# A normalization woven into a gated unit: one block for every four steps of dense work instead of three

## The chip, the cores and the metric

The kernel runs on one core of a Trainium2 chip. The metric is the device time of one execution in microseconds; of several executions the median counts. PE is the matmul engine (its weight loads are listed as PEld), DVE the vector engine, ACT the scalar engine, POOL the GpSimd engine, and SP issues most of the DMAs.

## The reference

The reference mixes two branches on one input `x` of 2048 rows and 640 columns, all in fp32:

```
g = sigmoid(sum(x * gate_w))                      # one number for each row
a = memory_attention(x; wq, wk, wv, wo, beta)     # 32 heads of 20, 4 chunks of 512 rows
b = (silu(x @ w1) * (x @ w3)) @ w2                # 1728 hidden columns
return g * a + (1 - g) * b
```

Within a chunk the attention is causal softmax over the chunk's own 512 rows. Beside it each chunk reads a memory, `phi(q) @ M / (phi(q) @ z)`, into which all earlier chunks have written `phi(k)^T @ v` and the sums of `phi(k)`. A sigmoid of `beta` mixes the two for each head, and `wo` projects the result.

## The kernel before, in words

The work is transposed: features lie on the 128 partitions and a chunk's 512 rows in the free dimension, so every matrix of 640 features has five blocks (`KB = 5`). For precision a factor is split into a high part and a low part, and a product is made of three matmuls per block of 128 (`PASSES`); a full product of one output block is 15 matmuls into one bank of PSUM. PSUM has eight banks, and all tiles in it are taken in turn from one list (`bank_tile`). A tile that gets a bank must wait until the last reader of the tile that had the bank before is done.

PE's order is the order in which the program is written; the other engines' instructions are ordered by a scheduler at build time. Two streams are merged into PE's order:

- The attention (`attention`, L761) goes over the heads in groups of four, in 40 slots each. In every group there is one big visit, with scores `s` (L602) for the row maxima, transposed scores `t` (L635) for the exponentials, and the product `o` (L655) with the values; and later a small visit with the rest of `s` and `t`. DVE reduces each `s` to row maxima (L609) and copies `o` out (L659). ACT makes the exponentials (L641), and POOL masks them (L645). After the small visit the maxima are split (L130 to L132), transposed on DVE (L620, `mr`) and sent into the next group's `qk` by two DMAs that ACT issues (L623).
- The dense work is a list of jobs, each a generator that yields after three matmuls or so, with the time in ns that they are reckoned at. A loop at the end of the kernel gives the dense jobs their share of each slot. At a big visit it first runs dense steps until no product is half done in its bank (`held` is empty).

The change concerns the segment of dense jobs that holds the output projection of the second chunk (chunk index 1). `ffn_up` (L502) is the gated unit: for one group of 128 hidden columns and the chunks 2 and 3 it makes a gate product `g` (15 matmuls, L253), a tanh on ACT (L514) and a product on DVE (L515), then an up product `u` (15 matmuls), a product on DVE (L521), a cast on ACT (L106) and the low part on POOL (L107). `normalize(1)` (L721) scales the attention output of chunk 1 block by block and adds the memory part; its loop is

```
ps = bank_tile(f"rr{c}_{b}")
nc.tensor.matmul(ps, sel[:, b * P:(b + 1) * P], rR, ...)     # L729: the factors, spread over rows
nc.vector.tensor_mul(o, oall[c][:, b].bitcast(F32), ps)      # L730
pt = bank_tile(f"gt{c}_{b}")                                 # L732
for qb in range(4):
    nc.tensor.transpose(pt[...], hi[...], ident)             # L734: the memory part, transposed
nc.vector.tensor_add(o, o, pt)                               # L735
nc.scalar.copy(hi, o)                                        # L736: high part, into gm
nc.vector.tensor_sub(oall[c][:, b], o, hi.bitcast(F32))      # L737: low part
yield 700
```

The output projection `op` (L805) then reads all five blocks of `gm` and `oall`, and is itself woven with the memory read `nd` (L348) of chunk 3. `braid(a, b, every)` (L856) merges two jobs: after every `every`-th step of `a` it runs one step of `b`, and at the end what is left of `b`. Weights are loaded by SP into two raw buffers (L163) and split on POOL (L174, L175) into six split buffers, each free when the last matmul on it is done.

## Time and profile before

| what | value |
|---|---|
| median of 3 runs | 1108.73 us (1108.67 to 1112.61) |
| the profiled execution | 1108.07 us, span 1106.4 us |
| granted clock of PE | 1.00 |
| matmul rows of the three dense products `g`, `u`, `f` | 840, 780, 820 |
| matmul rows of `s` and `o` | 512, 1024 |

In a row of the timeline stand the start in us from the span's start, the length in us, the engine, the line, the operation, the output and inputs by the program's names (without their numbers), the shape and the count of instructions merged; in brackets the engine's idle time just before and what ended it. The length of merged matmuls holds the tail of the last one, about 0.2 us, under which the next row has already begun. In a row of the waits stand who waited for whom, the sum in us, how often, and the longest. In a row of a stretch stand the stretch, its length, the busy times of PE, PEld, DVE, ACT and POOL with their counts, the granted clock, the share of the DMA engines and GB/s.

### The profile page before, as it was taken

What the parts mean: (1) busy time and instruction counts of PE and PEld (TensorE: products, weight loads), DVE (VectorE), ACT (ScalarE), POOL (GpSimd) and SP (SyncE); (2) the same over time, 40 slices, a digit from 0 to 9 for tenths busy, and PEclk for the clock granted to TensorE, in tenths of its full rate; (3) what the DMA queues carried; (4) which work ended last, traced back from release to release, by engine and by line L of the source; (5) the groups of instructions that cost most, each with busy time, mean ns of one, the idle gap of its engine ahead of it and who ended that gap; (6) DMA issues with size and microseconds to landing.
All of it is one profiled execution on the core that took longest, in us unless ns stands there. A gap on an engine that the chain in (4) does not pass through costs nothing.

```text
span 1106.4 us, 17867 instructions
## 1 busy us (share of the span) xinstructions
PE 1095.1 (99%) x6285; PEld 854.0 (77%) x6285; DVE 593.5 (54%) x1708; ACT 381.2 (34%) x826; POOL 583.3 (53%) x729
## 2 busy tenths in 40 slices
PE   9999999999999999999999999999999999999997
PEld 7988877777777777787977777777777777777786
DVE  5032564355555554366154678875557665551645
ACT  6244233343233122145244543424333332233120
POOL 5055556366366363565175547556764555565253
PEclk9999999999999999999999999999999999999999
DMA  8266943335165132535268967455654443432122
GB/s 314 102 212 220 281 117 82 95 82 127 47 164 125 57 78 94 156 98 191 96 202 271 287 204 193 103 157 138 166 139 111 103 104 90 117 105 86 52 79 95
DMA packets 87545, 153.20 MB, mean 138 GB/s; under 512 B 11584, under 2 KB 25184, under 8 KB 87456
## 3 DMA queue, kind: packets, MB, share of 16 engines
q1 hardware_dynamic: 63040, 106.30, 30.5%
q0 software_dynamic: 20384, 38.68, 15.6%
q10 hardware_dynamic: 4032, 7.08, 1.8%
q8 instruction: 50, 0.82, 0.3%
q14 instruction: 39, 0.32, 0.1%
HBM read 96.56 MB, written 54.54 MB: 137 GB/s over the span
## 4 chain that ended last, share of the span: by engine, by line
PE 94%; DVE 3%; ACT 1%; DMA 1%; issue 1%; ACTq 0%; SPq 0%; DVEq 0%
PE g L253 17%; PE u L253 16%; PE f L555 16%; PE k L253 6%; PE v L381 6%; PE op L805 6%; PE o L655 6%; PE q L253 5%; PE s L602 5%; PE t L635 4%; PE nd L348 1%; PE pm L445 1%; PE q L323 1%; DVE junk L609 1%; PE pkt L430 1%
## 5 line engine op out<-in xcount | busy, mean ns | idle before, releaser
L609 DVE CUSTOM_DVE_ANT_0 junk<-s,mask 128x256 bf16<-128x256 f32 (+3 forms) x512 | 250.3, 489 | 105.9 <-PE s L602 73.6
L641 ACT ACTIVATE P<-t 128x512 f32<-128x512 f32 (+1 forms) x384 | 172.4, 538 | 190.5 <-PE t L635 153.3
L253 PE MATMUL g<-X,W 128*128 128x512 f32 x840 | 208.7, 398 | 0.0
L175 POOL TENSOR_TENSOR W<-wr,W 128x640 fp32r<-128x640 f32 (+1 forms) x126 | 200.2, 1595 | 2.3
L174 POOL CAST W<-wr 128x640 fp32r<-128x640 f32 (+1 forms) x126 | 90.9, 726 | 208.9 <-PE f L555 47.0
L253 PE MATMUL u<-X,W 128*128 128x512 f32 x780 | 196.8, 399 | 0.0
L555 PE MATMUL f<-ht,W 128*128 128x512 f32 x820 | 196.6, 397 | 0.0
L645 POOL TENSOR_SCALAR_AFFINE_SELECT P<-P 128x256 f32<-128x256 f32 x192 | 94.0, 498 | 181.1 <-ACT P L641 180.7
L253 PEld LDWEIGHTS g<-X,W 128*128 128x128 f32 x840 | 156.0, 188 | 36.5 <-issue 0.4
L555 PEld LDWEIGHTS f<-ht,W 128*128 128x128 f32 x820 | 152.8, 188 | 36.5 <-DVE acc L536 0.4
L253 PEld LDWEIGHTS u<-X,W 128*128 128x128 f32 x780 | 144.1, 188 | 34.4 <-ACT P L641 0.3
L107 POOL TENSOR_TENSOR ht<-ft,ht 128x512 fp32r<-128x512 f32 x52 | 67.0, 1289 | 91.9 <-ACT ht L106 91.3
L579 POOL DMA_DIRECT2D qk<-qkd x128 | 83.3, 652 | 0.3
L602 PE MATMUL s<-qk 60*128 60x256 f32 (+3 forms) x512 | 78.2, 346 | 1.3 <-DVE fu L515 1.0
L253 PE MATMUL k<-X,W 128*128 128x512 f32 x300 | 77.0, 404 | 0.0
L655 PE MATMUL o<-P,vg 128*32 128x512 f32 (+3 forms) x1024 | 75.5, 436 | 1.4 <-DVE on L735 1.4
L514 ACT ACTIVATE ft<-g 128x512 f32<-128x512 f32 x52 | 31.1, 599 | 125.8 <-PE g L253 114.8
L381 PE MATMUL v<-W,X 128*128 128x320 f32 (+1 forms) x480 | 71.9, 311 | 0.4 <-ACT P L641 0.4
L515 DVE SCALAR_TENSOR_TENSOR fu<-ft,g 128x512 f32<-128x512 f32 x52 | 35.6, 685 | 68.3 <-ACT ft L514 59.2
L381 PEld LDWEIGHTS v<-W,X 128*128 128x128 f32 x480 | 71.0, 189 | 1.1 <-ACT P L641 0.6
L106 ACT CAST ht<-ft 128x512 fp32r<-128x512 f32 x52 | 32.2, 619 | 112.0 <-DVE ft L521 111.9
L563 DVE TENSOR_TENSOR acc<-f,acc 128x512 f32<-128x512 f32 x65 | 44.7, 689 | 44.8 <-PE f L555 44.6
(120 smaller groups left out, 1200.6 us busy)
## 6 DMA issues: line engine op xcount, KB each, us to landing
qk<-qkd POOLq DMA_DIRECT2D x128, 240.0 KB, 4.2
wr<-in_w_dram SPq DMA_DIRECT2D x80, 320.0 KB
qkd<-qs SPq DMA_DIRECT2D x20, 512.0 KB
qkd<-ks SPq DMA_DIRECT2D x20, 512.0 KB
od<-oq SPq DMA_DIRECT2D x32, 256.0 KB
wr<-in_wo_dram SPq DMA_DIRECT2D x20, 320.0 KB
vg<-vd SPq DMA_DIRECT2D x16, 336.0 KB
xr<-in_xT_dram SPq DMA_DIRECT2D x20, 256.0 KB
```

The source lines that it names most:

```text
L107: (lo or nc.gpsimd.tensor_sub)(dst[:, 1], src, dst[:, 0].bitcast(F32))
L174: nc.gpsimd.tensor_copy(w[:, 0, :n], raw[:, :n])
L175: nc.gpsimd.tensor_sub(w[:, 1, :n], raw[:, :n], w[:, 0, :n].bitcast(F32))
L253: nc.tensor.matmul(ps, w[:, a, kb * P:(kb + 1) * P], x[:, b, kb, :], start=n == 0, stop=n == 14)
L381: nc.tensor.matmul(ps[:, :n1 - n0], x[:, a, kb, lb * P:(lb + 1) * P], wvt[kb][:, b, n0:n1], start=n == 0, stop=n == 14)
L555: nc.tensor.matmul(ps, w, h, start=n == 0, stop=n == len(ms) - 1)
L579: here(nc.gpsimd.dma_start(t[64 * i:64 * i + RH], qkd[c][RH * (h + i):RH * (h + i + 1)]))
L602: nc.tensor.matmul(ps[i][:, o:o + w], q[:, qb * P:(qb + 1) * P], key[:, :w], start=n == 0, stop=n == len(todo) - 1, skip_group_check=True)
L609: nc.vector.tensor_tensor_reduce(out=junk[:, :w], in0=ps[i][:, o:o + w], in1=mask[:, L - w:], scale=1.0, scalar=-3.0e38, op0=ALU.add, op1= ...
L641: last["exp"] = nc.scalar.activation(pairs[2 * m + k]["P"][:, i, o:o + n], ps[i][:, b:b + n], AF.Exp, scale=SCALE)
L645: nc.gpsimd.affine_select(d, d, pattern=[[0, 2], [0, n], [1, P]], base=0, channel_multiplier=-1, compare_op=ALU.is_ge, fill=0.0)
L655: nc.tensor.matmul(ps[32 * i:32 * i + 32, kb * P:], heads[2 * p + i]["v"][:, kb], pairs[p + i // 2]["P"][:, i % 2, o:o + n], start=kb == 0 ...
```

## The change

In the segment of chunk 1's output projection, the gated unit `up[2]` of chunks 2 and 3 takes one block of `normalize(1)` after every four of its steps, where it took one after every three:

```
 o1, o2 = jobs_oproj(1)
-seg = [braid(up[2], o1, 3), braid(o2, job_read(3), 3, 1), job_down(B, 0), ...]
+seg = [braid(up[2], o1, 4), braid(o2, job_read(3), 3, 1), job_down(B, 0), ...]
```

`o1` is the normalization with its five blocks, `o2` the projection. Nothing else in the program is changed; what follows in the orders of the engines and in the turn of the banks follows from this number.

More of the change, by code (lines that the diff above doesn't have):

```diff
@@ L916, in gated_mix @@
     o1, o2 = jobs_oproj(1)
-    seg = [braid(up[2], o1, 3), braid(o2, job_read(3), 3, 1), job_down(B, 0), braid(chain(jobs_up(B, 1)), (0, load_memory(2)), 5)]
+    seg = [braid(up[2], o1, 4), braid(o2, job_read(3), 3, 1), job_down(B, 0), braid(chain(jobs_up(B, 1)), (0, load_memory(2)), 5)]
     segs.append((3 * H + LAG + 1, seg))
```

## The prediction

> **What bounds the kernel now.** I read the page first: its busy times and the chain that ended last.

> ```profile
> span 1106.4 us, 17867 instructions
> ...
> PE 1095.1 (99%) x6285; PEld 854.0 (77%) x6285; DVE 593.5 (54%) x1708; ACT 381.2 (34%) x826; POOL 583.3 (53%) x729
> ...
> PE 94%; DVE 3%; ACT 1%; DMA 1%; issue 1%; ACTq 0%; SPq 0%; DVEq 0%
> ```

> PE is busy for 1095.1 of 1106.4 us and carries 94% of the chain. The change adds and removes no matmul, so the time can move only by stalls of PE. The next view is the list of what PE waited for in the stretch from 680 to 780 us, where the second chunk's normalization lies. Then come the rows of PE in order of time.

> ```profile
> PE o L655 <- DVE on L735: 1.4, 1, 1.4
> ...
> 699.94 0.50 PE L602 MATMUL s<-qk 60*128 60x512 f32 x2
> 700.28 0.64 PE L635 MATMUL t<-qk 62*128 62x512 f32 x6
> 702.29 2.36 PE L655 MATMUL o<-P,vg 128*32 128x512 f32 x32 [1.37 <-DVE on L735]
> 704.59 0.50 PE L635 MATMUL t<-qk 62*128 62x512 f32 x2
> ...
> 706.01 1.66 PE L253 MATMUL g<-X,W 128*128 128x512 f32 x6
> 707.51 0.39 PE L729 MATMUL rr<-rR,sel 96*128 96x512 bf16 x1
> 707.74 0.60 PE L734 MATMUL gt<-ident,gm 128*128 128x128 f32 x4
> 708.09 2.34 PE L253 MATMUL g<-X,W 128*128 128x512 f32 x9
> 710.27 0.39 PE L729 MATMUL rr<-rR,sel 96*128 96x512 bf16 x1
> ...
> 710.86 1.63 PE L253 MATMUL u<-X,W 128*128 128x512 f32 x6
> 712.42 0.50 PE L602 MATMUL s<-qk 60*128 60x256 f32 x4
> 712.76 0.40 PE L635 MATMUL t<-qk 62*128 62x384 f32 x4
> 713.00 0.51 PE L602 MATMUL s<-qk 60*128 60x384 f32 x4
> 713.44 2.34 PE L253 MATMUL u<-X,W 128*128 128x512 f32 x9
> 715.61 0.62 PE L805 MATMUL op<-gm,W 128*128 128x512 f32 x2
> ...
> 718.40 0.85 PE L348 MATMUL nd<-Ms,pq 128*128 128x147 f32 x6
> 719.04 0.71 PE L805 MATMUL op<-gm,W 128*128 128x512 f32 x2
> ```

> One wait is to be seen: the PV product `o` (L655) stands still for 1.37 us until DVE has done an `on` addition (L735), because it gets the PSUM bank of that block's transposed memory part `gt`. Also to be seen is where the attention visits lie. A big one runs from 699.94 to 706.01, a small one from 712.42 to 713.44, and 6.4 us of dense work and of blocks 3 and 4 lie between them. The wait at `o` has its cause in DVE:

> ```profile
> 698.27 0.68 DVE L730 TENSOR_TENSOR on<-oall,rr 128x512 f32<-128x512 f32 x1
> 699.05 0.69 DVE L735 TENSOR_TENSOR on<-on,gt 128x512 f32<-128x512 f32 x1
> ...
> 701.46 0.68 DVE L735 TENSOR_TENSOR on<-on,gt 128x512 f32<-128x512 f32 x1
> 702.06 1.65 DVE L737 TENSOR_TENSOR oall<-on,gm 128x512 fp32r<-128x512 f32 x1
> ...
> 704.86 0.68 DVE L659 COPY oq<-o 128x512 f32<-128x512 f32 x1
> ...
> 709.46 0.68 DVE L735 TENSOR_TENSOR on<-on,gt 128x512 f32<-128x512 f32 x1
> ...
> 713.67 0.42 DVE L609 CUSTOM_DVE_ANT_0 junk<-s,mask 128x256 bf16<-128x256 f32 x1
> ...
> 716.60 0.68 DVE L521 SCALAR_TENSOR_TENSOR ft<-fu,u 128x512 f32<-128x512 f32 x1
> ...
> 718.35 0.08 DVE L609 DVE_READ_ACCUMULATOR2_ANT m<- 128x1 f32 x1
> 718.90 0.17 DVE L132 TENSOR_TENSOR ns<-m,nh 128x16 fp32r<-128x16 f32 x1 [0.48 <-ACT nh L131]
> 719.11 0.84 DVE L620 STREAM_TRANSPOSE mr<-ns 32x32 f32<-32x32 f32 x4
> ```

> The third block's L735 starts only at 701.46, behind older blocks and a row-maximum reduction. A 0.68 us operation of DVE gives way to the next after 0.60 (701.46 to 702.06).

> **The change part by part.** The order of instructions of the changed program shows what the braid moves. Blocks 0, 1 and 2 now come after 12 matmuls of `g2`, 9 of `u2` and 6 of `g3`. The planner then finishes `g3` before it opens the big visit, where before it was due after `u2`. So 15 matmuls, 9 of which take 2.17 us (713.44 to 715.61), pass from behind the big visit to before it: 3.6 us. Behind it only three matmuls of `u3` and block 3 are left before the small visit, and block 4 falls at the very end, behind all of `u3` and just before the output projection that consumes it. The banks rotate, so the tile that each one waits for changes for 27 tiles; from the next `o` on, every tile has the same predecessor as before.

> First, the wait at `o` goes: minus 1.37. The bank needed is still that of `gt` of block 2, but 9 matmuls of `g3` and the first part of the visit (699.94 to 700.92, about 1.0 us) stand between: 2.2 + 0.6 + 1.0 = 3.8 us from `rr` of block 2 to `o`. The two additions take 0.78 + 0.69 = 1.5 us (698.27, 699.05), and DVE's older work is done by then, since the blocks now follow one another by 12 matmuls, some 2.9 us. About 2 us are to spare.

> Second, a wait comes at the small visit. Call the end of `o` E (704.59 before). Without a wait PE needs 1.42 us to the end of the big visit (706.01), 0.75 for three matmuls (6 took 1.50, 706.01 to 707.51), 0.58 for block 3 (707.51 to 708.09), a step of 0.1, and 0.58 for the first eight matmuls of the visit (712.42 to 713.00): its last scores `s_4` are due at E + 3.4. Their banks are those of the last big scores, `s_1`. DVE takes up `oq` at E + 0.27 and needs nine steps: `oq`, two full reductions, four of `s_1` and both additions of block 3. Before, these nine ran without a gap from 704.86 to 709.46 + 0.60: 5.2 us. In the new order the last reduction closes them, so the bank is free at E + 5.5, and PE waits 5.5 − 3.4 = 2.1 us (in part already at the `t` scores before it). Before, the 6.4 us between the visits covered this; that cover is gone. The bounds: 1.3, if PE loses 0.2 us at each of four changes of group and so gives DVE time, and 2.4, if the step from addition to addition costs DVE its 0.18 gap (0.78 against 0.60) twice. I take 2.0, nearest to the row of the nine.

> Third, a wait comes at the output projection. `s_4` starts at E + 5.5. PE then does 0.44 (713.00 to 713.44), 12 matmuls of `u3` 2.9, block 4 0.58, twelve matmuls of `op` 2.79 (715.61 to 718.40), `nd` 0.64 (to 719.04), and at E + 12.85 wants `gm` of block 4. On DVE the small visit's reductions with one L737 and one L521 among them took 713.67 to 718.43; L521 now comes later, so 4.76 − 0.60 = 4.16, to E + 9.65. The maxima's split and L521 follow, 0.68 (718.43 to 719.11) + 0.60; then the transposes `mr` 0.84: E + 11.75. Block 4 stands behind all of this: 0.78 + 0.69 bring E + 13.2. ACT has its own queue ahead of the cast:

> ```profile
> 714.16 0.62 ACT L736 CAST gm<-on 128x512 fp32r<-128x512 f32 x1
> ...
> 719.99 1.08 ACTq L623 DMA_DIRECT2D qk<-mr  x2
> ...
> 701.89 1.28 POOL L107 TENSOR_TENSOR ht<-ft,ht 128x512 fp32r<-128x512 f32 x1 [5.76 <-ACT ht L106]
> 719.27 1.56 POOL L175 TENSOR_TENSOR W<-wr,W 128x640 fp32r<-128x640 f32 x1
> ```

> The two issues of L623 take 1.08 after `mr`, to E + 12.85, so the cast L736 waits for the addition alone: 13.2 + 0.05 + 0.62 = E + 13.9. PE waits 13.95 − 12.85 = 1.1 us. Two matmuls later (0.47) it wants the low part `oall` from L737. With a free DVE this ends 0.7 after the cast: a further 0.25. But L737 took 1.65 us where POOL's L107 ran from 701.89 to 703.17, and it ended at 703.71, 0.54 after that. Here POOL does L107 of `ht3` and then L175 of a weight. With L521 ending at E + 11.0 and a cast of 0.62 the chain is L107 to 12.95 and L175 to 14.5. L737 would start at 13.95 and end at 14.5 + 0.54 = 15.05, so PE waits 0.65 in place of 0.25. I take 0.65.

> [...]

> The weight split of POOL that waits for the end of `g3` starts earlier, and one weight load moves ahead of a store on SP's queue; both are consumed over 10 us later (the weight in `op` after `nd`), so I cost them at nothing. If that cover were gone, an L174 and L175 pair would show 0.7 + 1.56 us on PE. The descriptors of L579 stay in order between the same selects.

> The sum: −1.37 + 2.0 + 1.1 + 0.65 = +2.4 us. The profiled execution took 1108.07 us (its span of 1106.4 and 1.7 around it), so the changed one would take 1110.5. The median of before is 1108.73, 0.66 above that execution, and I forecast 1111.1 for the median. Behind the next `o` every engine's order and every bank's predecessor are as before, so the shift passes to the end unchanged. A measurement of this kernel tells about 0.5%, 5.5 us, from no change.

> **The rivals.** (1) Faster: the wait at `o` goes and nothing replaces it, because DVE reaches the maxima of the big visit sooner than the nine rows say. For it: DVE is only 54% busy. Against it: that is an average, and from 704.86 to 710.06 it had no gap. It decides if the nine steps take under 3.2 us. 1108.73 − 1.4 = 1107.4.

> (2) Half of it: the wait at the small visit comes, but gaps of PE's issue give DVE time, and block 4 is ready as `nd` ends; −1.4 + 1.3 + 0.3 leaves 1109.0.

> (3) Slower by over 0.5%: a stalled PE loses its clock. The first nine matmuls of the kernel took 0.45 us each against the 0.24 above:

> ```profile
> 1.26 4.02 PE L881 MATMUL warm<-zero 128*128 128x512 bf16 x9 [1.26 <-DVE zero L878]
> ...
> 699.90:702.30 2.40, 1.03 (x10) 0.76 (x10) 2.40 (x6) 2.09 (x5) 0.41 (x1) 1.00 0.01 3
> ```

> If each of the two new stalls brought 4.02 us of such work, half of that would be lost each time: 1111.1 + 4.0 = 1115.1. It decides at the length of a stall at which the granted clock falls; the wait of 1.37 us left it at 1.00 (the column behind the five busy times) and `o` after it took its 2.36. [...]

> That the change does nothing is ruled out by the order of instructions.

> **How the numbers follow.** My forecast has 0.75, rival 1 0.08, rival 2 0.13, rival 3 0.04. The forecast's own bounds are −1.37 + 1.3 + 0.6 + 0.25 = +0.8 and −1.37 + 2.4 + 1.6 + 0.9 = +3.5 (waits of `op` 0.5 either way of 1.1, and 0.25 or 0.9 for L737). The low end takes in rival 2 and a little below, 1108.7; the high end adds 0.6, by which a profiled run and the median differ: 1112.9. Only rival 3 lies over 0.5% slower, with 0.01 for what I have not seen; faster by over 0.5% has 0.01.

> **What would show it.** In the changed profile PE's wait at `o` on L735 near 702 us is gone and the big visit begins near 703.5. PE waits about 2 us in all inside the small visit, named after L609. It waits about 1 us at `op` for ACT's L736 and about half a microsecond for L737, and that L737 takes over 1 us beside L175. I am wrong if PE has no wait of over 0.5 us between the big visit and the second `op`, if the granted clock falls below 1.00 there, or if PE's waits outside 690 to 730 us differ by more than 1 us in sum.

## The result and the profile after

The changed kernel takes 1112.11 us (median of 20 executions, 1109.98 to 1115.29), the kernel before 1108.92 (20 executions, 1107.48 to 1112.61). The ratio is 1.0027 with a 95% interval of 1.002 to 1.0035, or 3.0 us more (2.2 to 3.9). The profiled execution took 1111.26 us. First the page of the changed kernel, its span and the busy times:

```profile
span 1109.5 us, 17865 instructions
...
PE 1095.0 (99%) x6285; PEld 852.9 (77%) x6285; DVE 592.9 (53%) x1708; ACT 381.4 (34%) x826; POOL 583.5 (53%) x729
```

PE is busy for 1095.0 us where it was 1095.1, and the span is 3.1 us longer: the same work with more standing still. What PE waited for from 690 to 735 us:

```profile
PE op L805 <- ACT gm L736: 1.4, 1, 1.4
PE s L602 <- DVE m L609: 0.9, 1, 0.9
PE op L805 <- DVE oall L737: 0.4, 1, 0.4
PE t L635 <- DVE m L609: 0.3, 1, 0.3
```

The one wait of before, `o` on L735, is not among them. Four others are. PE in order of time:

```profile
703.75 0.50 PE L602 MATMUL s<-qk 60*128 60x512 f32 x2
...
704.64 2.36 PE L655 MATMUL o<-P,vg 128*32 128x512 f32 x32
706.93 0.51 PE L635 MATMUL t<-qk 62*128 62x512 f32 x2
...
710.82 0.50 PE L635 MATMUL t<-qk 62*128 62x384 f32 x3 [0.32 <-DVE m L609]
712.23 0.51 PE L602 MATMUL s<-qk 60*128 60x384 f32 x4 [0.91 <-DVE m L609]
712.67 3.03 PE L253 MATMUL u<-X,W 128*128 128x512 f32 x12
...
715.54 0.39 PE L729 MATMUL rr<-rR,sel 96*128 96x512 bf16 x1
...
719.00 0.85 PE L348 MATMUL nd<-Ms,pq 128*128 128x147 f32 x6
721.23 0.70 PE L805 MATMUL op<-gm,W 128*128 128x512 f32 x2 [1.38 <-ACT gm L736]
722.29 0.50 PE L805 MATMUL op<-oall,W 128*128 128x512 f32 x1 [0.35 <-DVE oall L737]
...
727.82 2.36 PE L655 MATMUL o<-P,vg 128*32 128x512 f32 x32
```

The big visit runs straight through from 703.75. The small visit's last scores stand until 712.23, and `op` stands twice after `nd`. A listed wait leaves out the modelled tail of the matmul before it, about 0.2 us, so each is a little longer in truth. The rows of what PE waits for, on DVE, ACT and POOL:

```profile
707.07 0.69 DVE L659 COPY oq<-o 128x512 f32<-128x512 f32 x1 [0.88 <-PE o L655]
...
710.68 0.68 DVE L735 TENSOR_TENSOR on<-on,gt 128x512 f32<-128x512 f32 x1
...
712.09 0.08 DVE L609 DVE_READ_ACCUMULATOR2_ANT m<- 128x1 f32 x1
...
713.14 0.89 DVE L737 TENSOR_TENSOR oall<-on,gm 128x512 fp32r<-128x512 f32 x1
...
716.84 0.08 DVE L609 DVE_READ_ACCUMULATOR2_ANT m<- 128x1 f32 x1
...
718.09 0.83 DVE L620 STREAM_TRANSPOSE mr<-ns 32x32 f32<-32x32 f32 x4
718.95 0.69 DVE L730 TENSOR_TENSOR on<-oall,rr 128x512 f32<-128x512 f32 x1
719.75 0.69 DVE L735 TENSOR_TENSOR on<-on,gt 128x512 f32<-128x512 f32 x1
721.12 1.12 DVE L737 TENSOR_TENSOR oall<-on,gm 128x512 fp32r<-128x512 f32 x1 [0.68 <-ACT gm L736]
```

```profile
720.15 1.53 POOL L175 TENSOR_TENSOR W<-wr,W 128x640 fp32r<-128x640 f32 x1
```

```profile
706.00:724.00 18.00, 15.03 (x100) 10.93 (x89) 14.61 (x47) 5.99 (x15) 10.11 (x14) 1.00 0.55 135
```

The last reduction of `s_1` ends at 712.17 and the scores start at 712.23. The last block's L730 and L735 stand behind the maxima's split and `mr`, though `rr` of that block was done at 715.9. L737 lasts until 722.24, 0.56 us after POOL's L175. The granted clock in this stretch is 1.00.

**The measure used below.** PE's program is the same in all traces here up to this stretch, and yet they come to the `o` before it between 678.42 and 682.21 us. So beside the ratio, which is of many executions, I use the distance between two `o` rows of the one profiled execution: from the one just before the stretch (679.10 us before) to the third after it (745.50). In the expectations these are the third and the sixth big visit, counted from the one at 629.55 us. Before: 66.40 us. After: 679.40 to 748.26, 68.86 us, so +2.46.

### The profile page after: what moved, and what is told of

The parts are those of the page before. It is cut to its first block, busy times and chain, and to the rows that moved or that the text cites. A ratio compares the mean times of both kernels' runs of the same rounds, so it can differ in the third digit from the quotient of the medians.

```text
span 1109.5 us, 17865 instructions
## 1 busy us (share of the span) xinstructions
PE 1095.0 (99%) x6285; PEld 852.9 (77%) x6285; DVE 592.9 (53%) x1708; ACT 381.4 (34%) x826; POOL 583.5 (53%) x729
## 4 chain that ended last, share of the span: by engine, by line
PE 88%; DVE 4%; DMA 2%; POOL 2%; ACT 1%; issue 1%; SPq 0%; ACTq 0%; DVEq 0%; POOLq 0%
PE f L555 16%; PE g L253 15%; PE u L253 15%; PE k L253 6%; PE v L381 6%; PE o L655 6%; PE op L805 6%; PE q L253 5%; PE s L602 4%; PE t L635 3%; PE nd L348 1%; PE pm L445 1%; DVE junk L609 1%; PE q L323 1%; DMA wr<-in_w_dram 1%
## 5 line engine op out<-in xcount | busy, mean ns | idle before, releaser
L609 DVE CUSTOM_DVE_ANT_0 junk<-s,mask 128x256 bf16<-128x256 f32 (+3 forms) x512 | 250.5, 489 | 106.0 <-PE s L602 73.5
L253 PE MATMUL g<-X,W 128*128 128x512 f32 x840 | 208.6, 398 | 0.0
L174 POOL CAST W<-wr 128x640 fp32r<-128x640 f32 (+1 forms) x126 | 91.2, 728 | 212.2 <-PE f L555 46.9
L175 POOL TENSOR_TENSOR W<-wr,W 128x640 fp32r<-128x640 f32 (+1 forms) x126 | 200.0, 1593 | 2.2
L253 PE MATMUL u<-X,W 128*128 128x512 f32 x780 | 196.5, 399 | 0.0
L253 PEld LDWEIGHTS g<-X,W 128*128 128x128 f32 x840 | 155.9, 188 | 36.6 <-issue 0.4
L253 PEld LDWEIGHTS u<-X,W 128*128 128x128 f32 x780 | 144.0, 188 | 34.7 <-ACT P L641 0.3
L107 POOL TENSOR_TENSOR ht<-ft,ht 128x512 fp32r<-128x512 f32 x52 | 67.1, 1291 | 90.5 <-ACT ht L106 89.9
L579 POOL DMA_DIRECT2D qk<-qkd x128 | 83.5, 654 | 0.2
L602 PE MATMUL s<-qk 60*128 60x256 f32 (+3 forms) x512 | 78.1, 345 | 2.6 <-DVE fu L515 1.0
L253 PE MATMUL k<-X,W 128*128 128x512 f32 x300 | 77.0, 403 | 0.0
L655 PE MATMUL o<-P,vg 128*32 128x512 f32 (+3 forms) x1024 | 75.5, 436 | 0.1
L106 ACT CAST ht<-ft 128x512 fp32r<-128x512 f32 x52 | 32.2, 619 | 110.5 <-DVE ft L521 110.4
```

Source lines behind the costliest of these rows:

```text
L107: (lo or nc.gpsimd.tensor_sub)(dst[:, 1], src, dst[:, 0].bitcast(F32))
L174: nc.gpsimd.tensor_copy(w[:, 0, :n], raw[:, :n])
L175: nc.gpsimd.tensor_sub(w[:, 1, :n], raw[:, :n], w[:, 0, :n].bitcast(F32))
L253: nc.tensor.matmul(ps, w[:, a, kb * P:(kb + 1) * P], x[:, b, kb, :], start=n == 0, stop=n == 14)
L579: here(nc.gpsimd.dma_start(t[64 * i:64 * i + RH], qkd[c][RH * (h + i):RH * (h + i + 1)]))
L602: nc.tensor.matmul(ps[i][:, o:o + w], q[:, qb * P:(qb + 1) * P], key[:, :w], start=n == 0, stop=n == len(todo) - 1, skip_group_check=True)
```

## The experiments

| kernel | blocks of `normalize(1)` | distance against before | ratio to before, 95% |
|---|---|---|---|
| changed | one for four steps | +2.46 us | 1.0027 (1.0020 to 1.0035) |
| late_last | three; the last block after `u3` | +1.23 | 1.0007 (0.9997 to 1.0016) |
| same34 | four; the last block next to the fourth | +2.16 | 1.0009 (0.9999 to 1.0018) |
| apart6 | four; small visit six slots later | −0.09 | 1.0000 (0.9990 to 1.0010) |
| bank | three; one bank turned on before `o` | −0.02 | 0.9994 (0.9981 to 1.0007) |
| e2 | two | −0.04 | 0.9996 (0.9987 to 1.0004) |
| e1 | one | +3.33 | 1.0026 (1.0015 to 1.0036) |
| e4m2 | four, begun two steps earlier | +0.64 | 1.0008 (0.9998 to 1.0017) |
| e5 | five | +1.62 | 1.0028 (1.0016 to 1.0041) |
| e2_v | two; one low part from POOL to DVE | −1.07 | 0.9997 (0.9988 to 1.0006) |
| before_v | three; the same low part | +0.03 | 1.0005 (0.9993 to 1.0018) |
| after_v | four; the same low part | +3.89 | 1.0027 (1.0018 to 1.0035) |
| e3m2 | three, begun two steps earlier | −1.20 | 0.9985 (0.9976 to 0.9993) |

The theory in all of them is that of the prediction: DVE works its queue in order, and PE stands wherever the tile it needs is behind other things in that queue. One us is 0.0009 of the ratio. In the traces of same34, e1 and after_v the granted clock fell to half inside the stretch; that holds 1.5 to 1.6 us of each of these three distances, as the rows below show.

**late_last: the last block alone moved to the end.**

```
-braid(up[2], o1, 3)
+braid_at(up[2], o1, (3, 6, 9, 12, 20))   # block i after that many steps
```

> The kernel before with one part of the change alone: blocks 0 to 3 of the second chunk's normalization stay where they were (after every third step), block 4 alone goes behind all of u3, just before op. Theory (DVE's queue decides, in order: the wait at op comes only because the crowded visits had pushed DVE 5 us behind PE): the visits lie as before, so the last row maxima are done in time, gm of block 4 is cast by the time nd ends, and PE waits 0 to 0.3 us at op for L736; the wait of 1.4 us at o stays; time within 0.5 us of before. Rival (a block that stands right before its consumer costs its own latency, wherever DVE is): PE waits 1.1 to 1.7 us at op for L736 and L737 as in the changed kernel; 1.2 to 1.7 us slower than before.

Rows of DVE, POOL and PE:

```profile
722.07 1.70 DVE L737 TENSOR_TENSOR oall<-on,gm 128x512 fp32r<-128x512 f32 x1
```

```profile
721.69 1.54 POOL L175 TENSOR_TENSOR W<-wr,W 128x640 fp32r<-128x640 f32 x1
```

```profile
723.83 0.50 PE L805 MATMUL op<-oall,W 128*128 128x512 f32 x1 [1.03 <-DVE oall L737]
```

The wait at `o` stayed at 1.4 us. The high part was in time, but the low part L737 came behind `mr` and then ran for 1.70 us beside L175, ending 0.54 after it. So moving this one block cost 1.23 us in the distance: my figure for the theory (within 0.5 us) is missed, and the rival's (1.2 to 1.7) is met. What I had not reckoned with is the subtraction: with nothing of POOL's beside it, it takes 0.69 us (after_v below), so about 1.0 us of the wait is POOL's operation and not the block's own latency. By the distance, the place of block 4 alone makes about half of the change's cost; the ratio, 0.8 us more (−0.3 to 1.8), can't tell it from nothing.

**same34: the last block taken from the end of the changed kernel.**

```
-braid(up[2], o1, 4)
+braid_at(up[2], o1, (4, 8, 12, 16, 16))
```

> The changed kernel with block 4 taken back from the end: it goes together with block 3 after the 16th step, so PE does it right behind the small visit, 12 matmuls of u3 ahead of op. Theory: the wait inside the small visit stays at 1.2 to 2.0 us (nine DVE steps after o), the waits at op for L736 and L737 go; 1.3 to 1.8 us faster than the changed kernel, 0.5 to 1.2 slower than before. Rival (DVE's sum of work between o and op sets the time wherever the blocks stand): what op no longer waits comes back as a longer wait at the small visit or at the next t; as slow as the changed kernel, 2.4 to 3.2 us slower than before.

```profile
713.98 1.12 PE L734 MATMUL gt<-ident,gm 128*128 128x128 f32 x4 [0.22 <-DVE m L609]
714.74 4.21 PE L253 MATMUL u<-X,W 128*128 128x512 f32 x12
```

```profile
714.00:717.40 3.40, 3.40 (x10) 2.88 (x11) 3.37 (x10) 0.62 (x1) 1.40 (x3) 0.51 0.88 187
```

The two waits at `op` are gone, as the theory has it, but in this execution the distance fell by only 0.30 us. The rows say where the rest went. Twelve matmuls of `u3` took 4.21 us where they took 3.03 in the changed kernel, and from the start of `gt` to theirs it was 0.76 us, against 0.35 in the changed kernel's last block. From 714.0 to 717.4 the granted clock was 0.51 (the column behind the five busy times). Without these 1.6 us the gain would be 1.9. Over its 11 executions same34 is 1.0 us over the kernel before (−0.1 to 2.0), where the theory said 0.5 to 1.2 and the rival 2.4 to 3.2. So the work does not come back; the clock fell in the execution that was traced.

**apart6: the small visit moved away from the big one, in the changed kernel.**

```
+sm = SMALL + (6 if m == 19 else 0)      # this group's small visit six slots later
-todo = VISITS.get(n, ()) if ...
+todo = VISITS.get(SMALL if n == sm else -1 if n == SMALL else n, ()) if ...
...
-if n == SMALL and 0 <= m < NQUAD:
+if n == sm and 0 <= m < NQUAD:
...
```

> The changed kernel with the small visit of this one head group six slots later, so that nine matmuls of u3 lie between the two visits in place of three; blocks as in the changed kernel. Theory (the cover between the visits was lost): the wait inside the small visit falls from 1.2 in the listed waits to below 0.5 us; block 4 is no longer queued behind the maxima, so op waits below 0.5 us too; 0.5 to 1.4 us faster than before, since the wait at o is gone as well. Rival (DVE's work up to block 4 sets the time at op): the wait moves from the small visit to op, 2.5 to 3.5 us there; as slow as the changed kernel.

```profile
712.49 0.50 PE L602 MATMUL s<-qk 60*128 60x384 f32 x4 [0.29 <-DVE m L609]
...
719.73 0.50 PE L806 MATMUL op<-oall,W 128*128 128x512 f32 x1
```

(Lines behind L768 are one higher in this kernel.) This is the only listed wait left, and the distance is 2.55 us shorter than in the changed kernel. The loss depends on the dense work between the two visits, as the prediction's second step says. The further gain over the kernel before did not come: gaps of 0.3 to 0.5 us at `s`, `gt` and `op` remain (the last row starts 0.86 after `op` before it, where 0.55 is usual).

**bank: the kernel before, with the bank that `o` takes exchanged.**

```
+if p == 34:
+    free.append(free.pop(0))
 ps = bank_tile(f"o{p}")
```

> The kernel before, with one bank passed over in the turn just before that o, so that o gets the bank of u2 and not that of gt of block 2; nothing else is moved. Theory (DVE's backlog, not the bank, is behind the wait of 1.37 us): o starts some 1.4 us earlier, but a t or s of the same visit then waits about 1 us for the maxima of s_0, which DVE finished at 704.3 in the profile before; 0 to 0.5 us faster than before. Rival (the turn of the banks alone makes that wait): the whole 1.4 us are gained.

```profile
701.03 2.36 PE L657 MATMUL o<-P,vg 128*32 128x512 f32 x32 [0.17 <-DVE ft L521]
```

(Lines behind L651 are two higher in this kernel.) `o` started 1.2 us earlier, counted from the `o` before the stretch, and nothing was gained: `t` then waited 0.52 us for the maxima and `s` 0.22 for `oq`. The bank decides where PE's wait shows; DVE's backlog decides how long it is.

**e2 and e1: blocks closer together.** The edit is `braid(up[2], o1, 2)` and `braid(up[2], o1, 1)`.

> One block for every two steps: blocks 0 to 3 stand before the big visit, block 4 right behind it. Theory (VectorE's queue, in its order, decides; a block is 1.3 to 2.0 us of VectorE's work, two steps of TensorE are 1.3 us): the evictions of the blocks come ahead of the row maxima of both visits; the wait of o on the addition of block 3 becomes at most 1 us or goes, the small visit's scores and the product op wait under 0.3 us. Interval from o of the third big visit to o of the sixth: 0 to 1.4 us under that of the kernel before, -0.9. Rival (the wait of o only grows as the blocks are put closer, since the spacing is what VectorE can't follow): o waits 2 us or more, interval 0.7 us or more over that of the kernel before.

> One block for every step: all five blocks stand in the first fifteen products, ahead of the big visit by twelve products and more. Theory: TensorE gives out blocks every 0.9 us, VectorE takes 1.3 to 2.0 us for each and has caught up by the big visit's maxima; o waits under 1 us, nothing waits at the small visit or at op; interval from o of the third big visit to o of the sixth 0 to 1.4 us under that of the kernel before, -1.0. Rival (spacing decides): products and transposes of the blocks themselves wait for VectorE's evictions (the banks are taken in turn), 2 us and more in sum, interval 0.7 us or more over.

PE and POOL of e2:

```profile
719.19 0.50 PE L805 MATMUL op<-gm,W 128*128 128x512 f32 x1 [0.81 <-POOL W L175]
```

```profile
717.60 3.07 POOL L175 TENSOR_TENSOR W<-wr,W 128x640 fp32r<-128x640 f32 x2
```

In e2 no listed wait for DVE is left (two gaps of about 0.25 us at `s` remain), but the distance is the same as before, where −0.9 was expected: `op` now waits for a weight's low part, which stood on POOL behind L107 of `ht3`. Next late after DVE is POOL. e1 went the other way:

```profile
704.28 3.84 PE L655 MATMUL o<-P,vg 128*32 128x512 f32 x32 [1.40 <-DVE on L735]
```

```profile
703.46 0.68 DVE L735 TENSOR_TENSOR on<-on,gt 128x512 f32<-128x512 f32 x1
```

```profile
704.60:708.00 3.40, 3.40 (x32) 1.51 (x24) 0.90 (x3) 0.47 (x1) 0.72 (x2) 0.56 0.02 5
```

My figure for e1 is missed by 4 us. The rival's figure is met, but not its reason: the blocks' own products did not wait. `t` did for 0.5 us, `o` for 1.4 and, later, `op` for 0.8 on L175. PE gave out five blocks by 697.3, but DVE was at work with hardly a gap from 692.36 and reached the last L735 only at 703.46. The queue was the cause, but I had counted a block at 1.3 to 2.0 us and left the unit's own steps out. And again the clock fell, to 0.56 from 704.6 to 708.0, so that `o` took 3.84 us in place of 2.36.

**e4m2 and e5: the phase of the four, and five.** The edits are `braid(up[2], o1, 4, -2)` and `braid(up[2], o1, 5)`.

> One block for every four steps as in the changed kernel, but begun two steps earlier, so that the third block stands nine products before the big visit and the fourth between the two visits with twelve dense products behind it. Theory: the phase against the visits decides, not the spacing of four; o waits 0.3 to 0.8 us, the small visit and op under 0.4 us in sum; interval from o of the third big visit to o of the sixth 0.7 us under the kernel before (0 to -1.4). Rival (spacing of four itself costs): the interval stays within 0.5 us of the changed kernel's +2.5.

> One block for every five steps: the third block stands behind the big visit and the last two behind all dense work, right ahead of op. Theory: o waits for nothing, the small visit's scores wait 1 to 1.6 us as in the changed kernel, and op waits for the last cast and subtraction 2.5 to 3 us (two blocks of evictions behind m); interval from o of the third big visit to o of the sixth +3 to +4.5 us against the kernel before. Rival (the extra time of the changed kernel comes from the small visit alone): op waits no longer than in the changed kernel, 1.8 us, and the interval is +2 to +2.6.

PE of e4m2, then of e5:

```profile
713.27 0.38 PE L729 MATMUL rr<-rR,sel 96*128 96x512 bf16 x1 [0.61 <-DVE m L609]
714.32 0.65 PE L734 MATMUL gt<-ident,gm 128*128 128x128 f32 x4 [0.67 <-DVE m L609]
```

```profile
711.25 0.51 PE L602 MATMUL s<-qk 60*128 60x384 f32 x4 [0.91 <-DVE m L609]
...
718.05 0.70 PE L805 MATMUL op<-gm,W 128*128 128x512 f32 x2 [0.58 <-ACT ns L130]
719.08 0.50 PE L805 MATMUL op<-oall,W 128*128 128x512 f32 x1 [0.32 <-DVE oall L737]
```

e4m2 keeps the spacing of four and loses 1.8 us less than the changed kernel: the phase against the visits counts. The half of the theory that promised 0.7 us under before failed; the products of the last block then waited behind the small visit's maxima, 1.3 us in sum. In e5 the small visit waited as expected, but `op` less: the scheduler put both last blocks ahead of `mr` on DVE (L735 at 717.32, `mr` at 719.14), which I had not reckoned with. Its distance grew by 1.62, below my 3 to 4.5 and below the rival's 2 to 2.6, while its ratio means 3.1 us (1.8 to 4.5); the difference is not explained by its one trace.

**e2_v, before_v, after_v: one subtraction moved from POOL to DVE.**

```
-split(ht, t)
+split(ht, t, lo=nc.vector.tensor_sub if (c, j) == (3, 2) else None)   # L107 of ht3
```

> One block for every two steps, and the low part of the gated product of chunk 3, unit 2 (L107, 1.28 us on GpSimd) is subtracted on VectorE instead. In the kernel with one block for every two steps the product op waited 0.8 us for the low part of a weight piece (L175), which stood behind that L107 in GpSimd's queue. Theory (with VectorE's waits gone, GpSimd's queue is next late): the wait of op on L175 goes, VectorE is idle there for over 1 us and hides its 0.7 us; interval from o of the third big visit to o of the sixth -0.7 to -1.4 us against the kernel before, -1.0, and the time about 0.1% under it. Rival (the weight piece is late for its own reasons, its buffer or its load): the wait stays at 0.6 us or more, interval 0 to -0.3.

> The kernel before, with that one low part subtracted on VectorE instead of GpSimd: the control for the run with two steps. Theory: o still waits 1.4 us for the addition of block 3, op waits for nothing as before, VectorE has room for 0.7 us behind the maxima of the small visit: interval within 0.3 us of the kernel before. Rival (taking work off GpSimd gains by itself, as GpSimd's reads block VectorE's L737): 0.4 us or more under it.

> The changed kernel, with that one low part subtracted on VectorE instead of GpSimd. It puts 0.6 us into VectorE's queue between the multiply and the addition of the last block, and lets the weight piece's L175 on GpSimd start 1.3 us sooner, so that it is over when the last block's subtraction L737 starts. Theory: op waits for the cast 0.6 us longer (1.4 becomes 2.0), the subtraction takes 0.69 us instead of 1.12 and op's wait for it is 0.1 us or less; interval +2.3 to +2.9 us against the kernel before. Rival (the subtraction's length has nothing to do with GpSimd's running operation): it stays over 1 us, op waits 0.4 us for it as well, interval +3 us or more.

In e2_v PE has no listed wait in the stretch, and the distance is 1.07 us under before: POOL's queue was what e2 waited for. The median does not show it (the interval of the ratio reaches from −1.3 to +0.7 us). before_v, the control, moved the distance by 0.03. In after_v, DVE, PE and the stretches:

```profile
720.88 0.69 DVE L737 TENSOR_TENSOR oall<-on,gm 128x512 fp32r<-128x512 f32 x1 [0.68 <-ACT gm L736]
```

```profile
720.99 0.85 PE L805 MATMUL op<-gm,W 128*128 128x512 f32 x2 [1.80 <-ACT gm L736]
```

```profile
718.00:721.40 3.40, 1.60 (x11) 1.25 (x9) 2.67 (x6) 0.80 (x2) 0.00 (x0) 1.00 0.37 105
721.40:724.80 3.40, 3.40 (x10) 2.50 (x9) 1.68 (x5) 0.00 (x0) 1.17 (x1) 0.50 0.45 121
```

With L175 over at 717.49, L737 took 0.69 us instead of 1.12, and `op` did not wait for it: the length of that subtraction is made by POOL's running operation. The wait for the cast grew by 0.4, near the 0.6 expected. The distance grew more than expected (2.3 to 2.9), since after this longer wait the clock stood at 0.50 for 3.4 us. Nine matmuls of `op` took 3.79 us from 720.99 on; in the kernel before they took 2.23 from 719.04 to 721.27. Without these 1.56 us the distance would be +2.33, and the ratio over its executions, 1.0027, is that of the changed kernel.

**e3m2: the spacing of before, begun two steps earlier.** The edit is `braid(up[2], o1, 3, -2)`.

> One block for every three steps as in the kernel before, begun two steps earlier. Blocks 0 to 2 stand ahead of the big visit, by nine products and more, block 3 right behind it, block 4 three products ahead of the small visit. Theory (VectorE's queue): o waits under 0.3 us, the small visit's scores 0.3 to 1 us since block 4's evictions come just ahead of its maxima, op for nothing; interval 0 to -1 us against the kernel before, -0.5. Rival (the spacing of three steps costs what it costs, the phase does nothing): o or the block's own products wait 1.4 us in sum as before, interval within 0.3 us.

```profile
702.23 2.36 PE L655 MATMUL o<-P,vg 128*32 128x512 f32 x32
...
725.23 2.36 PE L655 MATMUL o<-P,vg 128*32 128x512 f32 x32
```

```profile
690.00:730.00 40.00, 39.97 (x264) 29.36 (x261) 33.00 (x98) 16.69 (x38) 20.98 (x28) 1.00 0.41 121
```

PE is busy for 39.97 of 40 us and nothing is listed as waiting. The distance is 1.20 us shorter, a little more than the 0 to 1 expected, and the kernel takes 1107.36 us against 1108.68, a ratio of 0.9985 (0.9976 to 0.9993): the one version here whose interval lies under 1.

## Why the prediction was right

The forecast was 1111.1 us; the measured 1112.11 lies in its range. By its own steps:

- **The wait at `o` goes, −1.37.** It is gone, and the big visit began at 703.75 where near 703.5 was said. From the start of `t` to that of `o` it was 2.01 us before (700.28 to 702.29) and is 0.55 now, so 1.46 were gained.
- **The small visit, +2.0.** With E at 706.93, the last scores were due at E + 3.4 and came at 712.23, E + 5.30, against E + 5.5 forecast: 1.9 us, of which the list shows 0.32 and 0.91. The chain of nine steps on DVE was the right one, and apart6 shows that more work between the visits removes the wait.
- **The cast for `op`, +1.1.** `nd` ended for PE at 719.64, E + 12.7, and `op` began at E + 14.30: 1.6 us. The term was too small by 0.5. The last maximum came at E + 10.0 and not E + 9.65, in part since the L737 in between held DVE for 0.81 us (713.14 to 713.95) and not 0.60; the rest of the 0.5 is PE being 0.15 earlier. That the block stands behind `mr` is as forecast.
- **L737, +0.65.** In the kernel before this matmul starts 0.55 us after the first two of its group (719.04 to 719.59). `op` so wanted L737 at 721.78 and began at 722.29: 0.5. L737 ended 0.56 us after L175, forecast 0.54. after_v took L175 away and with it the wait.
- **The sum, +2.4.** The distance says +2.46 in the profiled execution. Counted from start to start of the same rows of PE before and after, the terms are −1.46, +1.83 (the eight matmuls of the small visit took 0.58 us and now 2.41), +1.59 and +0.51: 2.47.

Of the 3.1 us by which the spans differ, 0.30 was there before the stretch, and a wait of 0.5 us for `qkd` at 952 us came after it.

The prediction named waits outside 690 to 730 us that differ by more than 1 us as a sign against it. They do differ, by 1.6 us in sum, and the sign was badly chosen: 1.1 of it lies ahead of the stretch, where PE's two programs are the same, and moved `o` there by only 0.30.

**Rivals 1 and 2** fall with these steps: the nine steps took 5.1 us (707.07 to 712.17), not under 3.2, and `gm` of block 4 was not ready as `nd` ended.

**Rival 3, the lost clock,** was put at 0.04. That was my estimate: the one stall measured by then, of 1.37 us, had left the clock at 1.00, and no run had shown at what length above that it falls. Here the reasoning failed, though not the forecast. In the changed kernel's profile the clock stayed at 1.00 up to the end of PE's work at 1103.87 us. But in after_v, same34 and e1 it fell to half after waits of the same kind, at a cost of 1.5 to 1.6 us each, not the 2 us assumed. That it did not fall in the changed kernel's trace seems to be luck: the last section shows where its waits lay. The mean granted clock tells something of the other executions. It also holds the half clock at the end, when PE has nothing left to do (0.50 from 1106.43 us on in that profile), so traces without a fall under PE's work have means of 0.998 to 1.000. Of the 20 executions of the changed kernel 8 have 0.997 or less, of the 97 of the kernel before in the three sets of experiments 6. So a part of the changed kernel's executions lost clock under work; their median is 1112.7 us, that of the other 12 is 1111.7. Where it was lost no trace shows: in those of late_last and same34 the clock also fell once between 7 and 13 us, where PE's programs are the same.

Adding the terms one by one holds as long as the clock does: in the trace of same34 the terms of `op` were taken away, and a fall of the clock took most of the gain back.

## What to carry to other kernels

Before spreading side work thinner, look at which in-order queue finishes it and at what that queue must do next: here DVE's half-idle average hid that a block given out just before a row of reductions is finished only after them. A fixed spacing is a poor knob: the best version came from the phase against the visits (two steps earlier at the same spacing), and by the ratio no spacing tried without it beat the kernel before. And waits of the matmul engine that add up to 1.4 to 1.9 us within 3.4 us were followed here by 1.5 to 1.6 us more in clock, so their price is not their length alone.

## What the runs showed of the hardware

```profile
717.31:720.73 3.42, 2.54 (x14) 2.03 (x13) 2.86 (x8) 0.94 (x3) 1.82 (x2) 1.00 0.01 3
720.73:724.14 3.41, 2.55 (x11) 1.84 (x12) 2.60 (x5) 0.36 (x1) 0.95 (x1) 1.00 0.52 159
718.90:722.30 3.40, 1.66 (x11) 1.06 (x9) 2.58 (x5) 0.62 (x1) 2.77 (x2) 1.00 0.15 47
```

With the grid 1.6 us later the same waits would have left one period with 1.66 us; that the clock would then have fallen is likely from the three falls, but not shown. Nor need such a period be empty: the one in same34 with PE busy for 2.00 of 3.41 us was followed by a fall.

**L737, a subtraction of two SBUF tiles, ended about half a microsecond after POOL's operation where it started beside one,** whatever its own start. In the rows of DVE and POOL of 12 of the traces, L737 (L739 in bank) starts so 22 times between 695 and 723 us, and ends 0.54 to 0.56 us after the operation of POOL each time. In after_v, with nothing of POOL's beside it, it was 0.69 us long. In the changed kernel there is a case where it started first: it kept its 0.69, and POOL's was longer. L174 took 0.88 us from 703.88 on, beside an L737 from 703.49 to 704.18, and 0.71 from 715.77 on. What the half microsecond consists of, and which of POOL's accesses holds L737 up, no run shows.
